# Four K and Q loads moved from the SP queue to GpSimd's queue, between the loads of two weight matrices

## The chip, the cores and the metric

The kernel runs on one core of one Trainium2 chip. The metric is the time of one execution in device microseconds (us), as the median of several runs; the lower the better. The profile shows one execution, in which the hardware profiler recorded every instruction and every DMA packet.

## The reference

Four batches, eight heads, 768 positions and a head size of 64. Causal attention in which every query sees only the six chunks of 32 keys that score highest by a bound, followed by a two-layer network with ELU:

```python
k_min, k_max = k_chunks.min(3), k_chunks.max(3)          # (B, H, 24, D): 24 chunks of 32 keys
ub = sum(maximum(q * k_min, q * k_max), axis=-1)         # bound of every query with every chunk
ub = where(causal, ub, -1e9)
sel = the 6 chunks with the largest ub                   # per query
scores = where(sel & causal, q @ k.T / sqrt(D), -1e9)
x = (softmax(scores) @ v) as (3072, 512)                 # heads side by side
h = x @ w_in                                             # w_in 512 x 2048
out = where(h > 0, h, exp(min(h, 0)) - 1) @ w_out        # w_out 2048 x 512
```

## The kernel before

**Tiling.** The 3072 rows of x are done in eight units of 384. Units 0 and 1 each take 192 positions of batch 0 and the same 192 of batch 1: unit 0 ("p") the positions 0 to 191, for which all chunks that may be seen are among the six, so that no selection is needed, and unit 1 ("s") the positions 192 to 383. The later units are halves of one batch. For each unit the kernel loads K, Q and V, turns K and Q on TensorE (PE), forms minima and maxima of the K chunks (kst) and the bounds, selects, scores, takes exp, multiplies with V, and turns the result into four tiles xt. The two-layer network (`mlp`) of a unit follows: for each of 16 blocks of 128 columns of w_in, four matmuls (L872) accumulate over the four xt; ACT takes exp (L879), GpSimd or DVE subtracts 1 (`m`, L881), DVE joins both sides (`gT`, L885). Then, for three groups of 128 rows, sixteen matmuls with w_out (L896), in four steps of four, one for each piece of w_out.

**The order of work.** Every step is an operation of a graph with a number. The string `ORDER` holds the program's order, written out: three characters for each operation, the first for the engine (P for PE, A for ACT, D for DVE, G for GpSimd, which the profile calls POOL, S for SP) and two for the operation's number. `PLACES` holds the buffer of each tile in the same order. Each engine runs its instructions in this order, and waits on semaphores where an operand isn't ready. SP issues most DMAs; its issues are instructions of its queue as well.

**The loads near the change.** In `prep_pair(b, u, G)` the K and Q rows of one unit come in as two tiles each of class `f` (96 positions x 8 heads x 64 values, float32, 192 KB: 768 runs of 256 bytes), at L308 through the helper `dma`, on SP. Only the Q of unit 0 is loaded by GpSimd, with a cast to bfloat16 (L388). The weights are loaded by GpSimd with a cast as well: w_in in two pieces of eight blocks (`load_w_in`, L295; `GmB` and `GmC` in `ORDER`), w_out in four pieces of four blocks (`load_w_out`, L301; `GmD` to `GmG`). The four loads that the change moves are `S2M` and `S2N` (K) and `S2O` and `S2P` (Q), the cast `G0Y`. The first w_out piece is used by the first L896 of unit 0, the second by the fifth to eighth block, and so on. Everything that GpSimd issues goes through one software queue (q0 in the profile); what SP issues goes through a hardware queue (q1); both are served by the same 16 DMA engines.

**Who uses the moved tiles.** K of unit 1 of batch 1 is turned by PE at L423 (`kT1s0`, `kT1s1`, four transposes each), Q likewise (`qT1s0`, `qT1s1`). The first V tile of batch 1 (128 rows) is cast to bfloat16 into `vext` by GpSimd at L337 (`vcast`). L749 scores unit 1, L613 forms the bounds of all queries with the chunks, L374 is the subtraction of K's minima from the maxima.

Of the kernel before, what the change touches and what calls it, by code (L numbers as in the profile page):

```python
# [34 lines left out]
PE, ACT, DVE, POOL, SP = "PE", "ACT", "DVE", "POOL", "SP"  # L35
# [4 lines left out]
G0vS0UD00D01PjXA02D09PjYS0sPjZG0wD06Pj-D0iPj+S0uPk0G0aPk1D0oS0rPk2A0TD0jG0kPk3A0tPk4S0XD03G04Pk5  # L40
Pk6Pk7Pk8D05G0bP1mD0lG0cG0WP1hP1nPk9S2dG0eG0pG0VPkaPkbPkcP0KA0OD0PPkdPkeG0nG0gG0fS2fPkfPkgD0qD0m
P18P0RP0IG0dD0SD0MP0BS0zA0JA1cP0+P1iD0CS0xA0FD19P1oP1jS0ZD10D1aD13S2eD0LS2gA1qA1pA15D11GmBP16P1f
P1sS2MA1lD0ND0DD0GS2PS2tP1xA1gD17G0AG08G0yP1wA1kD12P1rP1yS2ND0QP1tA1AGmCP1VA1vA1zD0-P1BP1CP1WD1D
P24P23D25A1uG0YP27P28D26G07D1EG1eP1PP1GD29P1QP1-D1XA2aG0EP1ZD1+D20P1MP1FP1LG2hD1HP2bG1bG2QD1RP2z
D1IA1YP2mD2AP1JD2nP2HP21S2GD1ND1OA1SP1TA2qD2oS2OA1KD22P2uD1UA2cPmXG0HG2sA2ID2BG0hD2pG2CPn3AmYDmZ
Dm-Pm+An4PmTGn5An0D2vA2JGmDPmPD2wAmUDbqP3jDn6Gn1Dn2A2DS2RAmQGmVPn7A2rG14D3lA1dPmHG2xAn8D3kD3mGmE
A2yPmLD3nPnfGn9DmWAmMGmRDnaAmIPnDA2KGmNDmSPnrPnzAngGmFD3oA2FAnEGmJDnhPnjD3pGmGDmOA3qA3sPnnDniG3r
AnsP3FDmKAnoGnFPnbA3GGntDnGPnNAnAGnpDnuAncGnBS2kDnqAnkP3+PnvGndA40DnCS2iP3HDneP36D38A3IP2VD37P3Z
# [52 lines left out]
SwSPwJPwKDwLSwMPwVPwWAwXSwYPwZPw-Pw+Px0Dx1Sx2  # L101
"""
PLACES = """
010234561723809400a15670000116732123410154351712367920340512011326120372504022630201740451602060
0001712105100321222310106020041302422105371001210657208104429601a202b10225c63d5074344173e0675174
232002354f0131811a051702149562710202334657702101110353224400271111415003200024301667235013082223
6211124241g0321703025031511642080210211a14023024060172b50d501200217001e9903040645563645270036705
340231510610a143324462420c4518036175460720352160242050221360512703003437015067105025412256406301
2015462720241f034232126300182750369851002011b24115422110702d5117600120301271a12022e1g1502921a044
5364106150341652360311745073a7480420141216521017436560746000200310074351642530340701436007410610  # L110
42322012500347220410676023221c798035120b001246202d1701400505612260110022020f000241743012305621e0
071112221931755412a2640316137544050011601a47135720640203353013120721001117220g041122026531002711
74c02263021d1670105693482300e122f61101154501822304b674310511676271325701101360217051295706272306
123706204523075601020103360271112010022300042411320a621132020237250411ce0252361030170751421bg120
20612350204814010012f010001652733027095310264575302140352735620410026321622347203011031211521200
6712400d341281052302217b02012a13620c211102507243023ef7110g61154420673450256564172631401101225514
# [53 lines left out]
def kernel(  # L170
# [25 lines left out]
    def ap(b):  # L196
        return store[b.cls][b.slot]
# [44 lines left out]
    def short(b):  # L242
        return ap(b)[:, 0:256].bitcast(BF16)
# [61 lines left out]
    def dma(dst_src, writes, reads, name, engines=(SP,)):  # L305
        def emit(e):
            d, s_ = dst_src()
            eng[e].dma_start(out=d, in_=s_)  # L308
        return g.op(name, engines, emit, reads=reads, writes=writes, dma=True)
# [68 lines left out]
    def prep_pair(b, u, G):  # L378
# [4 lines left out]
        if G == 0:  # L383
            for n, cls, src in (("k", "f", k), ("q", "f", q)):
                for x in range(2):
                    ff[b, n, x] = buf = Buf(cls)
                    if (n, u) == ("q", 0):
                        g.op(f"wq{b}{x}", (POOL,), lambda e, buf=buf, x=x: nc.gpsimd.dma_start(  # L388
                            out=short(buf)[0:T96].rearrange("p (h d) -> p h d", d=D),
                            in_=q[b, :, T96 * x:T96 * (x + 1)].rearrange("h p d -> p h d")),  # L390
                            writes=[(buf, i) for i in range(NG)], dma=True)
                        continue
                    for y, (h0, h1) in enumerate(((0, 4), (4, 8)) if (b, u) == (0, 0) else ((0, 8),)):
                        dma(lambda buf=buf, src=src, x=x, h0=h0, h1=h1: (
                                ap(buf)[0:T96, D * h0:D * h1].rearrange("p (h d) -> p h d", d=D),
                                src[b, h0:h1, t0 + T96 * x:t0 + T96 * (x + 1)].rearrange("h p d -> p h d")),
                            [(buf, i) for i in range(h0 // 4, h1 // 4)], [], f"ld{n}{b}{'ps'[u]}{x}{y}",
                            (SP, ACT) if u == 0 and n == "k" else (SP,))
        kf, qf = [[ff[b, n, x] for x in range(2)] for n in "kq"]

        def turned(bk):
# [524 lines left out]
    for u in range(2):  # L926
        for b in range(2):
            for G in range(NG):
                prep_pair(b, u, G)
        if u == 1:  # L930
            for b in range(2):
                select(b, 0)
        else:
            for b in range(2):
                for G in range(NG):
                    score_first(b, G)
        for r in range(NPAIR):
            attend_pair(u, r)
# [63 lines left out]
```

## Time and profile before

| | us |
|---|---|
| median of 3 runs | 280.8 |
| lowest and highest | 280.65 and 281.0 |
| the profiled execution | 280.54 |
| its span, first to last instruction | 278.8 |

The mean TensorE clock granted in the profiled execution was 0.994 of full speed. In the timeline rows the first number is the start in us from the span's start, the second the duration; the bracket at the end tells how long the engine sat idle before it and what ended that. A row of a DMA issue tells the time of the issuing instruction; the time from issue to landing stands in the DMA view, as the last number of a row. In the DMA view the rows of queues tell packets, MB and the time that the packets took as a share of 16 engines' time. In the table by stages each row is a stretch of the span, with the busy time of every engine, the granted clock, and the DMA engines' busy share and rate.

### The profile page before, as it was taken

What the parts mean: (1) busy time and instruction counts of PE and PEld (TensorE: products, weight loads), DVE (VectorE), ACT (ScalarE), POOL (GpSimd) and SP (SyncE); (2) the same over time, 40 slices, a digit from 0 to 9 for tenths busy, and PEclk for the clock granted to TensorE, in tenths of its full rate; (3) what the DMA queues carried; (4) which work ended last, traced back from release to release, by engine and by line L of the source; (5) the groups of instructions that cost most, each with busy time, mean ns of one, the idle gap of its engine ahead of it and who ended that gap; (6) DMA issues with size and microseconds to landing.
All of it is one profiled execution on the core that took longest, in us unless ns stands there. A gap on an engine that the chain in (4) does not pass through costs nothing.

```text
span 278.8 us, 6961 instructions
## 1 busy us (share of the span) xinstructions
PE 266.1 (95%) x2458; PEld 163.2 (59%) x2458; DVE 219.2 (79%) x655; ACT 216.7 (78%) x491; POOL 127.9 (46%) x255
## 2 busy tenths in 40 slices
PE   7587999999999999999999999999999999999995
PEld 4354555785466855576655555666655555665553
DVE  4897976889978999889998999578797698424931
ACT  2577886889699998999999859886968579982620
POOL 8874944258422665321685736212541346310410
PEclk9989999999999999999999999999999999999999
DMA  9999999999228899975965489417600410033002
GB/s 146 203 198 206 229 196 202 224 221 254 49 66 203 238 237 182 209 177 114 195 160 126 104 211 224 77 39 129 173 4 0 60 39 4 14 125 95 16 12 101
DMA packets 103219, 38.07 MB, mean 137 GB/s; under 512 B 95120, under 2 KB 98448, under 8 KB 103184
## 3 DMA queue, kind: packets, MB, share of 16 engines
q1 hardware_dynamic: 95696, 32.75, 56.9%
q0 software_dynamic: 6304, 4.59, 10.7%
q10 hardware_dynamic: 1184, 0.30, 0.5%
q8 instruction: 19, 0.31, 0.5%
q14 instruction: 16, 0.13, 0.2%
HBM read 30.41 MB, written 6.29 MB: 132 GB/s over the span
## 4 chain that ended last, share of the span: by engine, by line
PE 74%; DVE 8%; POOL 5%; ACT 5%; DMA 4%; issue 3%; POOLq 0%; DVEq 0%; ACTq 0%
PE bank L896 26%; PE bank L872 24%; PE bank L803 10%; PE bank L854 5%; DMA w_in_sb<-in_moe_w_in_dram 4%; PE bank L613 3%; PE bank L564 2%; DVE gT L885 2%; ACT pt L818 1%; ACT e L879 1%; PE bank L914 1%; POOL m L881 1%; PE bank L775 1%; POOL f L388 1%; PE bank L749 1%
## 5 line engine op out<-in xcount | busy, mean ns | idle before, releaser
L872 PE MATMUL bank<-xt,w_in_sb 128*128 128x384 bf16 x512 | 89.1, 326 | 1.0 <-DMA w_in_sb<-in_moe_w_in_dram 0.9
L896 PE MATMUL bank<-w_out_sb,gT 128*128 128x512 bf16 x368 | 89.3, 379 | 0.0
L881 POOL TENSOR_SCALAR m<-e 128x384 f32<-128x384 f32 x100 | 52.9, 537 | 61.2 <-ACT e L879 51.1
L885 DVE SCALAR_TENSOR_TENSOR gT<-bank,m 128x384 bf16<-128x384 f32 x128 | 65.7, 549 | 9.5 <-POOL m L881 8.3
L879 ACT ACTIVATE e<-bank 128x384 f32<-128x384 f32 x128 | 59.1, 493 | 15.7 <-PE bank L872 12.9
L872 PEld LDWEIGHTS <-w_in_sb 128*128 128x128 bf16 x512 | 49.3, 98 | 35.6 <-issue 3.1
L818 ACT ACTIVATE pt<-bank 128x384 bf16<-128x384 f32 (+1 forms) x144 | 67.1, 547 | 3.6 <-PE bank L803 2.5
L896 PEld LDWEIGHTS <-gT 128*128 128x128 bf16 x368 | 34.6, 97 | 36.1 <-issue 2.3
L803 PE MATMUL bank<-rhs,lhs 96*128 96x384 bf16 (+2 forms) x240 | 42.8, 293 | 1.0 <-DVE on L667 0.5
L835 POOL TENSOR_TENSOR pt<-pt,tri 128x256 bf16<-128x256 bf16 (+1 forms) x18 | 16.4, 915 | 37.8 <-ACT pt L822 23.9
L803 PEld LDWEIGHTS <-lhs 96*128 96x128 bf16 x240 | 21.7, 97 | 13.9 <-issue 1.0
L854 PEld LDWEIGHTS <-pt 128*128 128x128 bf16 x576 | 21.0, 97 | 3.6 <-ACT pt L818 0.2
L854 PE MATMUL bank<-vext,pt 128*128 128x65 bf16 x576 | 22.1, 193 | 0.0
L667 DVE TENSOR_TENSOR on<-bank,rcp 128x384 bf16<-128x384 f32 (+1 forms) x37 | 18.7, 510 | 1.3
L324 ACT ACTIVATE o<-bank 128x512 f32<-128x512 f32 (+1 forms) x14 | 8.1, 588 | 13.0 <-PE bank L896 10.1
L326 POOL CAST rhs<-qt 64x384 bf16<-64x384 f32 x24 | 12.6, 531 | 12.1 <-ACT qt L324 11.0
L657 DVE RECIPROCAL rcp<-bank 128x6 f32<-128x6 f32 (+1 forms) x40 | 7.2, 185 | 12.5 <-PE bank L854 9.0
L371 DVE TENSOR_REDUCE kst<-bank 128x12 f32<-128x384 f32 x32 | 16.4, 547 | 0.7 <-ACT kt L324 0.4
L326 DVE COPY o<-bank 128x512 f32<-128x512 f32 (+1 forms) x11 | 7.2, 665 | 11.9 <-PE bank L896 9.9
L835 DVE TENSOR_TENSOR pt<-pt,tri 128x512 bf16<-128x512 bf16 (+1 forms) x30 | 11.5, 398 | 5.5 <-ACT pt L822 3.7
L324 ACT ACTIVATE rhs<-qt 64x384 bf16<-64x384 f32 x28 | 14.2, 518 | 0.5
L822 ACT ACTIVATE pt<-bank 128x512 bf16<-128x512 f32 x24 | 14.1, 604 | 0.7 <-PE bank L803 0.5
(105 smaller groups left out, 338.1 us busy)
## 6 DMA issues: line engine op xcount, KB each, us to landing
f<-in_v_dram SPq DMA_DIRECT2D x22, 256.0 KB, 4.6
out_dram<-o SPq DMA_DIRECT2D x21, 256.0 KB, 3.6
f<-in_q_dram SPq DMA_DIRECT2D x18, 256.0 KB, 4.8
f<-in_k_dram SPq DMA_DIRECT2D x18, 256.0 KB, 4.6
kc<-in_k_dram SPq DMA_DIRECT2D x8, 384.0 KB, 4.0
w_in_sb<-in_moe_w_in_dram POOLq DMA_DIRECT2D x2, 1024.0 KB, 12.2
w_out_sb<-in_moe_w_out_dram POOLq DMA_DIRECT2D x4, 512.0 KB, 9.3
f<-in_k_dram SPq DMA_DIRECT2D x5, 192.0 KB, 6.7
```

Of the source, the lines that this page charges most:

```text
L324: nc.scalar.activation(out=dst, in_=src, func=AF.Copy)
L326: eng[e].tensor_copy(out=dst, in_=src)
L667: nc.vector.tensor_tensor(out=ap(on)[:, 0:nt].rearrange("p q h d -> p h q d"), in0=view()[:, :, :, 0:D], in1=ap(rcp)[:, :, 0:nt].to_broadc ...
L803: nc.tensor.matmul(ap(banks[hd])[:, o + pc:o + pc + wd], lhsT=apl(ls, G)[0:96, pr, hd, P * kb:P * (kb + 1)], rhs=ap(rs)[0:96, hd, c0 - HS ...
L818: lambda e, hd=hd, pt=pt, banks=banks, wtot=wtot: nc.scalar.activation(out=ap(pt)[:, hd, PAD:PAD + wtot], in_=ap(banks[hd])[:, 0:wtot], fu ...
L835: eng[e].tensor_tensor(out=view, in0=view, in1=tri[:, 64:64 + P].rearrange("p (a b w) -> p a b w", a=1, b=1) .to_broadcast([P, 2, len(dg), ...
L854: nc.tensor.matmul(view()[:, hd, qi, :], lhsT=ap(pt)[:, hd, P * qi + off:P * qi + off + P], rhs=ap(vx[b])[:, kb, 2 * r + hd, :], start=(kb ...
L872: nc.tensor.matmul(ap(bank)[:, 0:HS], lhsT=w_in_sb[:, kk, P * fc:P * (fc + 1)], rhs=ap(xT[i, kk]), start=(kk == 0), stop=(kk == NKK - 1))
L879: g.op(f"e{i}.{fc}", (ACT,), lambda e, eb=eb, bank=bank: nc.scalar.activation(out=ap(eb), in_=ap(bank)[:, 0:HS], func=AF.Exp), reads=[(ban ...
L881: g.op(f"m{i}.{fc}", (POOL, DVE), lambda e, eb=eb, mb=mb: eng[e].tensor_scalar(out=ap(mb), in0=ap(eb), scalar1=-1.0, scalar2=1.0, op0=AOT. ...
L885: nc.vector.scalar_tensor_tensor(out=ap(gt), in0=ap(bank)[:, 0:HS], scalar=0.0, in1=ap(mb), op0=AOT.max, op1=AOT.min),
L896: nc.tensor.matmul(ap(bank), lhsT=ap(gts[fc])[:, P * tt:P * (tt + 1)], rhs=w_out_sb[:, fc, :], start=(fc == 0), stop=(fc == NFC - 1))
```

## The change

The four loads of K and Q for unit 1 of batch 1 are issued by GpSimd, directly behind its issue of the second w_in piece, K first. The cast of batch 1's first V tile, which GpSimd ran just behind that w_in issue, runs just ahead of it. In SP's order the four issues are gone, and what stood behind them moves up: two copies of constants into `lhs`, then the V loads of unit 1. GpSimd's order around the place is then: first w_in piece, two V casts, the third V cast, second w_in piece, K, K, Q, Q, and on as before. PE, DVE and ACT keep their orders. Some tiles of class `f` change places (`PLACES`), since the loads ask for buffers in another order.

```diff
-P1sS2MA1lD0ND0DD0GS2PS2tP1xA1gD17G0AG08G0yP1wA1kD12P1rP1yS2ND0QP1tA1AGmCP1VA1vA1zD0-P1BP1CP1WD1D
-P24P23D25A1uG0YP27P28D26G07D1EG1eP1PP1GD29P1QP1-D1XA2aG0EP1ZD1+D20P1MP1FP1LG2hD1HP2bG1bG2QD1RP2z
-D1IA1YP2mD2AP1JD2nP2HP21S2GD1ND1OA1SP1TA2qD2oS2OA1KD22P2uD1UA2cPmXG0HG2sA2ID2BG0hD2pG2CPn3AmYDmZ
+P1sA1lD0ND0DD0GS2tP1xA1gD17G0AG08G0yP1wA1kD12P1rP1yD0QP1tA1AG0YGmCG2MG2NG2OG2PP1VA1vA1zD0-P1BP1C
+P1WD1DP24P23D25A1uP27P28D26G07D1EG1eP1PP1GD29P1QP1-D1XA2aG0EP1ZD1+D20P1MP1FP1LG2hD1HP2bG1bG2QD1RP2z
...
-                            (SP, ACT) if u == 0 and n == "k" else (SP,))
+                            (SP, ACT) if (u, n) == (0, "k") else (POOL,) if (b, u) == (1, 1) else (SP,))
```

More of the change, by code (lines that the diff above doesn't have):

```diff
@@ L42 @@
 P18P0RP0IG0dD0SD0MP0BS0zA0JA1cP0+P1iD0CS0xA0FD19P1oP1jS0ZD10D1aD13S2eD0LS2gA1qA1pA15D11GmBP16P1f
-P1sS2MA1lD0ND0DD0GS2PS2tP1xA1gD17G0AG08G0yP1wA1kD12P1rP1yS2ND0QP1tA1AGmCP1VA1vA1zD0-P1BP1CP1WD1D
-P24P23D25A1uG0YP27P28D26G07D1EG1eP1PP1GD29P1QP1-D1XA2aG0EP1ZD1+D20P1MP1FP1LG2hD1HP2bG1bG2QD1RP2z
-D1IA1YP2mD2AP1JD2nP2HP21S2GD1ND1OA1SP1TA2qD2oS2OA1KD22P2uD1UA2cPmXG0HG2sA2ID2BG0hD2pG2CPn3AmYDmZ
+P1sA1lD0ND0DD0GS2tP1xA1gD17G0AG08G0yP1wA1kD12P1rP1yD0QP1tA1AG0YGmCG2MG2NG2OG2PP1VA1vA1zD0-P1BP1C
+P1WD1DP24P23D25A1uP27P28D26G07D1EG1eP1PP1GD29P1QP1-D1XA2aG0EP1ZD1+D20P1MP1FP1LG2hD1HP2bG1bG2QD1R
+P2zD1IA1YP2mD2AP1JD2nP2HP21S2GD1ND1OA1SP1TA2qD2oA1KD22P2uD1UA2cPmXG0HG2sA2ID2BG0hD2pG2CPn3AmYDmZ
 Dm-Pm+An4PmTGn5An0D2vA2JGmDPmPD2wAmUDbqP3jDn6Gn1Dn2A2DS2RAmQGmVPn7A2rG14D3lA1dPmHG2xAn8D3kD3mGmE
@@ L103 @@
 PLACES = """
[L104 to L113, printed above, removed]
+010234561723809400a15670000116732123410154311236725790034051201132612037250402263020174451602060
+0001712105100321222310106020041302422105371001210657208104429601a206b10225c23d5074344173e0675174
+232002354f0131811a051702147562710202334659702101110353224400671111415003200024301267235013082223
+6211124241g0321703025031511642080210211a14023024060172b50d501200217001e7903040645563645270036905
+340231510210a143364462420c4518036175460720352160242050221360512703003437015067105025412256406301
+2015462920241f034232126300182750367851002011b24115422110702d5117600120301271a12022e1g1502921a044
+5364106150341652360311745073a9480420141216521017436560746000200310074351642530340701436007410610
+42322012500349220410676023221c778035120b001246202d1701400505612260110022020f000241743012305621e0
+071112221931755412a2640316137544050011601a47135720640203353013120921001117220g041122026531002711
+74c02263021d1670105673482300e122f61101154501822304b674310511676271325701101360217051295706272306
 123706204523075601020103360271112010022300042411320a621132020237250411ce0252361030170751421bg120
```

## The prediction

> **What bounds the kernel now.** I read the page first, then the table by stages, TensorE's (PE's) waits, its timeline, and last the DMA queues.
>
> ```profile
> span 278.8 us, 6961 instructions
> ...
> PE 266.1 (95%) x2458; PEld 163.2 (59%) x2458; DVE 219.2 (79%) x655; ACT 216.7 (78%) x491; POOL 127.9 (46%) x255
> ```
>
> ```profile
> core 0: us, PE busy (x) PEld busy (x) DVE busy (x) ACT busy (x) POOL busy (x), PEclk, DMA share, GB/s
> 9.88:13.30 3.42, 1.82 (x25) 1.09 (x26) 3.42 (x9) 1.54 (x4) 2.67 (x21) 1.00 1.51 184
> 13.30:16.71 3.41, 3.00 (x24) 1.47 (x23) 3.40 (x8) 2.14 (x5) 3.30 (x7) 0.50 1.36 182
> 20.12:23.54 3.42, 2.14 (x28) 1.76 (x26) 3.13 (x10) 3.27 (x12) 1.84 (x5) 1.00 1.13 205
> 23.74:30.00 6.26, 6.22 (x64) 3.58 (x65) 4.85 (x18) 4.80 (x11) 4.27 (x9) 1.00 1.16 225
> 30.00:35.30 5.30, 5.09 (x33) 2.91 (x31) 5.27 (x18) 4.21 (x11) 4.38 (x8) 1.00 1.27 213
> 35.30:41.30 6.00, 5.35 (x40) 3.04 (x38) 4.95 (x11) 5.26 (x13) 3.38 (x8) 1.00 1.22 196
> 41.30:80.00 38.70, 38.69 (x381) 23.93 (x382) 33.46 (x114) 31.25 (x69) 18.53 (x36) 1.00 0.85 174
> ```
>
> PE is busy 95% of the span. From 23.74 us on it hardly rests: 6.22 of 6.26 us, 5.09 of 5.30, 5.35 of 6.00, then 38.69 of 38.70. A microsecond that PE stands still after 23.74 us is therefore a microsecond of the total, except what can be taken from the 0.65 us that are idle between 35.3 and 41.3.
>
> PE's waits from 23 us to the end hold one row that names a DMA, and the timeline shows where it is:
>
> ```profile
> PE bank L872 <- DMA w_in_sb<-in_moe_w_in_dram: 0.9, 1, 0.9
> ```
>
> ```profile
> 23.78 3.42 PE L872 MATMUL bank<-xt,w_in_sb 128*128 128x384 bf16 x20 [0.87 <-DMA w_in_sb<-in_moe_w_in_dram]
> ...
> 28.09 6.02 PE L872 MATMUL bank<-xt,w_in_sb 128*128 128x384 bf16 x36
> ...
> 34.68 0.81 PE L872 MATMUL bank<-xt,w_in_sb 128*128 128x384 bf16 x4
> 35.33 1.03 PE L896 MATMUL bank<-w_out_sb,gT 128*128 128x512 bf16 x4
> ...
> 37.37 1.08 PE L423 MATMUL bank<-ident_f,f 96*128 96x96 f32 x8
> ...
> 38.72 1.89 PE L896 MATMUL bank<-w_out_sb,gT 128*128 128x512 bf16 x8
> 41.23 0.40 PE L749 MATMUL bank<-rhs,lhs 96*128 96x128 bf16 x3 [0.61 <-ACT lhs L324]
> ...
> 42.55 0.49 PE L423 MATMUL bank<-ident_f,f 96*128 96x96 f32 x4
> ```
>
> The first use of w_in is at 23.78, the first of w_out at 35.33. The eight L423 at 37.37 turn the moved K; those of the moved Q begin at 42.55. Now GpSimd's queue, and the time from issue to landing of each w_in piece and of the first two w_out pieces:
>
> ```profile
> 13.46 0.81 POOL L295 DMA_DIRECT2D w_in_sb<-in_moe_w_in_dram  x1
> ...
> 15.71 0.80 POOL L295 DMA_DIRECT2D w_in_sb<-in_moe_w_in_dram  x1
> 16.54 0.72 POOL L337 TENSOR_SCALAR vext<-f 128x512 bf16<-128x512 f32 x1
> ...
> 18.33 0.21 POOL L374 TENSOR_TENSOR kst<-kst 128x12 f32<-128x12 f32 x1
> ...
> 22.33 0.50 POOL L326 COPY lhs<-kt 64x384 bf16<-64x384 bf16 x1 [1.33 <-ACT kt L324]
> ...
> 26.33 0.83 POOL L301 DMA_DIRECT2D w_out_sb<-in_moe_w_out_dram  x1
> ...
> 29.11 0.78 POOL L301 DMA_DIRECT2D w_out_sb<-in_moe_w_out_dram  x1
> ```
>
> ```profile
> w_in_sb<-in_moe_w_in_dram POOLq DMA_DIRECT2D x1, 1024.0 KB, 10.3
> ...
> w_in_sb<-in_moe_w_in_dram POOLq DMA_DIRECT2D x1, 1024.0 KB, 14.1
> ...
> w_out_sb<-in_moe_w_out_dram POOLq DMA_DIRECT2D x1, 512.0 KB, 8.3
> ...
> w_out_sb<-in_moe_w_out_dram POOLq DMA_DIRECT2D x1, 512.0 KB, 8.9
> ```
>
> Issue plus landing time: w_in at 23.8 and 29.8, w_out at 34.6 and 38.0. They come one after the other, 6.0, 4.8 and 3.4 us apart, though two were issued 2.3 us apart: GpSimd's queue (q0) hands them over in order. The margins are thin. Each block of L872 is four matmuls; the ninth block needs the second w_in piece and starts at 28.09 + 12 x 6.02/36 = 30.1 (piece there 29.8); the first w_out piece is there 0.7 us before its use at 35.33.
>
> **The change part by part.** *Four loads join q0 between w_in and w_out.* Each is 96 x 8 rows of 256 bytes, together 3072 packets. How fast q0 moves such rows beside the SP queue (q1), from the stages at 5 to 7 us and 8 to 11 us (the four Q loads with cast, 256-byte reads), from 18 to 27 us (w_in on q0), and q1 alone from 48 to 55 us:
>
> ```profile
> q0 software_dynamic: 1339, 0.17, 131.4%
> q1 hardware_dynamic: 734, 0.18, 55.7%
> ...
> q0 software_dynamic: 1516, 0.19, 99.8%
> q1 hardware_dynamic: 1771, 0.44, 74.1%
> ...
> q0 software_dynamic: 803, 1.61, 94.5%
> q1 hardware_dynamic: 785, 0.20, 16.9%
> ...
> q1 hardware_dynamic: 6225, 1.57, 105.7%
> ```
>
> q0 got 670 packets per us in the first stage and 505 in the second. 3072 of them take 4.6 or 6.1 us; I take 5.4, the middle, since both rows are the same kind of transfer under the same competition. The ends: alone on the engines at q1's 889 per us, 3.5 us; half of that rate, 6.9 us. q1 will not be empty: while w_in runs it got 785 packets in 9 us, one for each of q0's 803, so whatever SP puts there instead of K and Q is still there at 29.8.
>
> The first w_out piece then lands at 29.8 + 5.4 + 3.4 = 38.6 (3.4 us as between the two pieces that follow each other without a pause; its issue at 26.33 is early enough). PE reaches its L896 at 35.33 as before and stands 3.3 us. Ends: 29.8 + 3.5 + 3.4 = 36.7, a stand of 1.4; 29.8 + 6.9 + 4.8 = 41.5, a stand of 6.2. Behind this L896 in PE's order stand four L872 of the last block, so ACT's exp, GpSimd's m and DVE's gT of that block, and the L423 transposes with DVE's kst and ACT's kt behind them; nothing on PE can pass it.
>
> The Trainium skill speaks for the low end: "DMA: Bandwidth & Descriptors", Queues, rings and completion order, says that an engine takes a whole packet, typically 9 to 17 descriptors, from one ring before it turns to the next, so short rows of q0 would go out many at a turn. By that rule the loads come near the 3.5 us and the sum becomes a stand of 1.4; the rows (803 against 785; 1339 against 734) show at most about two for one, and the rows decide.
>
> *What is late next.* The second w_out piece lands 3.4 later, 42.0. PE asks for it in the second half of the L896 row at 38.72, at 38.72 + 0.95 + 3.3 = 43.0: in time. K (first half of q0's 5.4 us) is there by 32.5, Q by 35.2, against 37.37 and 42.55: in time even without the stand.
>
> *What is won back.* The 0.61 us before L749 at 41.23 are a wait for ACT's copy, which waited for DVE's kst, which waited its turn behind gT work. During the stand DVE empties that work. I take 0.5 back; bounds 0 and 0.65, the stage's whole idle time.
>
> *The clock.* The stretch from 9.88 with PE busy 1.82 of 3.42 us is followed by one at clock 0.50; the stretch from 20.12 with 2.14 busy is not. A stand of 3.3 us lies in two such stretches at most, so one of them has at least 1.65 idle, 1.76 busy, under the first row. A stretch of 3.41 us at half clock loses up to 1.7 us of PE's work; I take 1.2, as part of that stretch is waiting anyway. Bounds 0 (a short stand) and 1.7.
>
> *GpSimd's time.* The four issues cost as the four Q loads at the start did:
>
> ```profile
> L388 POOL DMA_DIRECT2D f<-in_q_dram x4: 772/783/1000, 1.4 to 6.6; - x4
> ```
>
> 4 x 0.78 = 3.1 us from about 17.2. Behind them stand a tri select, lhs copies, the kst subtractions from 18.33 on and small memsets. Before the copy of 22.33 GpSimd waited 1.33 us for ACT, so at most 1.8 of the 3.1 us are left there. The batch-0 bound product on PE, which needs kst, comes after the 20 L872 of 23.78, not before 27.1: room for that. Cost 0; without the cover up to 3.1 us on kst. The Trainium skill, "SBUF — State Buffer", Who interferes with whom, says that DVE in its two-port mode locks GpSimd out of writing descriptors, and the page gives 3.1 us in place of 0.62 for such a transfer; four of these, an estimate by that page, would be 12 us and eat the cover. This trace does not show it: w_in's issues took 0.81 and 0.80 while DVE was busy 3.40 of 3.41 us.
>
> *The V cast ahead of w_in.* 0.72 us (row 16.54), its data there already, since it started without a wait. The second w_in piece is issued 0.7 later, at 16.4, still 7 us before the first has landed, and q0 is in order: cost 0. If q0 ran dry instead: 0.7.
>
> *SP's queue.* Four issues go, among them this one:
>
> ```profile
> 19.71 6.60 SPq L308 DMA_DIRECT2D f<-in_q_dram  x1
> ```
>
> SP reaches the econst copies and V loads up to ten us earlier. They change no PE wait, as none from 23 us on names them: gain 0. Nor does w_in profit much: q1 stays filled, with 256 packets of 768 bytes now first. Were the first piece earlier, PE could not start before its last xt:
>
> ```profile
> 22.78 0.61 DVE L326 COPY xt<-bank 128x384 bf16<-128x384 bf16 x2
> ```
>
> That ends at 23.39, so the gain is at most 0.4 us; slower econst rows may as well cost 0.4. I take 0.
>
> **The sum**: +3.3 - 0.5 + 1.2 = +4.0 us. The profiled execution took 280.54 us (span 278.8 and 1.7 around it), so 284.5; the three runs have their median at 280.8, 0.3 higher: 284.8.
>
> **The rivals.** *No stand to speak of* (chance 0.14): q0's rows go out faster than any row shows, or PE is later than thought; a stand under 1.3 us, no half clock, 0.5 won back: -0.2 to +0.8, about 281.1. Against it: even 889 per us gives 1.4.
>
> *Faster* (0.08): q0 is not strictly in order, the loads slip in beside w_in, and w_out is there by 35.3; then only the 0.4 us at 23.78 count: 280.4. It decides at one point, w_out's landing before 35.3; w_in's landings 6.0 us apart for issues 2.3 apart speak against it.
>
> *GpSimd is held at its own queue* (0.10): SP's issue of 6.60 us shows what a full queue does. With w_in and 3072 rows behind it, GpSimd's third or fourth issue could last until about 26 to 29; kst comes late for the bound product at 27.1 (about 3 us of PE), w_out is issued later still. +6 to +8, about 288. Against it: no GpSimd issue in these rows exceeds 1.0 us, though none had as much queued.
>
> **How the numbers follow.** The forecast has 0.68. Its range: stand 1.4, 0.5 back, no half clock: +0.9, 281.7; stand 4.8 (6.9 us for the loads), nothing back, 1.7 of clock: +6.5, 287.3. I give 281.6 to 287.4, which leaves out the faster case, most of the held queue and part of the first rival, together 2 in 10. 0.2% (0.56 us) is about what a measurement here can tell from no change. Slower by more: 0.68 + 0.10 + 0.07 of the first rival; within: 0.05 of it; faster: 0.08 + 0.02: 0.85, 0.05, 0.10.
>
> **What would show it.** Right: four K and Q rows on GpSimd's DMA issues at about 0.78 us each; the first w_out piece landing some 12 us after issue in place of 8.3; a PE wait of about 3 us at L896 near 35.3, named after w_out's DMA; a half-clock stretch after it; 41 to 80 us as full as now. Wrong: L896 starting at 35.3 without a wait refutes the sum; a long GpSimd issue near 18 to 20 us means the held queue; a long wait at L872 near 30 means that w_in, not w_out, pays.

## The result, and the profile after

| | changed | before |
|---|---|---|
| median of 11 runs, us | 282.46 | 280.92 |
| lowest to highest, us | 281.63 to 285.12 | 280.27 to 281.84 |
| profiled execution, us | 281.63 | 280.54 |

The ratio is 1.0058, 95% interval 1.0038 to 1.0077: slower by 1.5 us, where +4.0 was forecast. The direction and the range held; the size did not. Ratios and intervals here and below come from all executions of both kernels but a few slow ones, so they need not equal the quotient of the medians.

TensorE's (PE's) waits and its timeline of the changed kernel, as in the prediction. The waits' columns are total, times and longest, in us.

```profile
PE bank L896 <- DMA w_out_sb<-in_moe_w_out_dram: 1.7, 1, 1.7
PE bank L872 <- DMA w_in_sb<-in_moe_w_in_dram: 0.9, 1, 0.9
...
PE bank L749 <- ACT lhs L324: 0.6, 1, 0.6
```

```profile
23.32 3.42 PE L872 MATMUL bank<-xt,w_in_sb 128*128 128x384 bf16 x20 [0.86 <-DMA w_in_sb<-in_moe_w_in_dram]
...
36.69 1.02 PE L896 MATMUL bank<-w_out_sb,gT 128*128 128x512 bf16 x4 [1.66 <-DMA w_out_sb<-in_moe_w_out_dram]
...
38.64 0.82 PE L423 MATMUL bank<-ident_f,f 96*128 96x96 f32 x8
...
42.25 0.40 PE L749 MATMUL bank<-rhs,lhs 96*128 96x128 bf16 x3 [0.61 <-ACT lhs L324]
```

The new wait is where the prediction put it: the first L896, ended by the first w_out piece. It lasts 1.66 us, not 3.3. The 0.61 us before the later L749 has stayed. And PE begins L872 0.46 us earlier than in the execution of before (23.32 against 23.78).

The rows of GpSimd's DMA issues, by the DMA view; the last number is the median time from issue to landing. The first row is of the second w_in piece, the last of the first w_out piece.

```profile
w_in_sb<-in_moe_w_in_dram POOLq DMA_DIRECT2D x1, 1024.0 KB, 12.8
f<-in_k_dram POOLq DMA_DIRECT2D x2, 192.0 KB, 13.1
f<-in_q_dram POOLq DMA_DIRECT2D x2, 192.0 KB, 13.7
...
w_out_sb<-in_moe_w_out_dram POOLq DMA_DIRECT2D x1, 512.0 KB, 10.8
```

And GpSimd's timeline:

```profile
16.30 0.79 POOL L295 DMA_DIRECT2D w_in_sb<-in_moe_w_in_dram  x1
17.10 1.58 POOL L308 DMA_DIRECT2D f<-in_k_dram  x2
18.67 1.54 POOL L308 DMA_DIRECT2D f<-in_q_dram  x2
...
22.12 0.95 POOL L326 COPY lhs<-kt 64x384 bf16<-64x384 bf16 x2
```

The four issues took 3.12 us (3.1 predicted), and at 22.12 GpSimd is level with before: nothing was paid there. The second w_in piece lands at 16.30 + 12.8 = 29.1, the four loads by 33.3 (single landings 30.1, 31.2, 32.2, 33.3), the first w_out piece at 36.6. So, by the landings, the loads took 4.2 us, not 5.4, and were complete one by one in order, 1.05 us apart.

Why they were faster shows in the table of queues of the page (packets, MB, share). First the changed kernel's row, then that of before:

```profile
q0 software_dynamic: 6560, 5.37, 12.0%
```

```profile
q0 software_dynamic: 6304, 4.59, 10.7%
```

The four loads brought 0.78 MB in 256 more packets, not 3072. Of those, by the packet records, 192 carry 4096 bytes, sixteen rows of 256 bytes each, and 64 are of 4 bytes. The packets of 4096 bytes start between 27.4 and 32.1 us, the first of them before w_in has landed, and w_out's first one starts at 31.7. In the stretch in which q0 sent hardly anything else (28.6 to 30.6 us), SP's rows, still one per packet, went out one for each packet of q0:

```profile
q0 software_dynamic: 129, 0.39, 94.1%
q1 hardware_dynamic: 127, 0.03, 13.3%
```

So the two queues took turns packet by packet, as beside w_in in the prediction (803 against 785). But a packet of the loads held 4096 bytes and one of q1 256: q0 moved 0.39 MB beside 0.03 MB on q1.

No half-clock stretch follows the wait. The profiler's stretches of 3.41 us around it, in the columns of the table by stages, and the later stage:

```profile
32.80:36.21 3.41, 1.99 (x13) 0.96 (x11) 3.01 (x7) 2.88 (x7) 2.45 (x6) 1.00 1.21 195
36.21:39.62 3.41, 2.94 (x27) 2.19 (x27) 1.79 (x4) 2.02 (x5) 1.47 (x3) 1.00 1.22 196
...
41.30:80.00 38.70, 38.07 (x378) 23.50 (x377) 33.10 (x112) 31.20 (x68) 18.57 (x36) 1.00 0.87 176
```

From 42 us on the kernel runs 1.0 us behind before, and ends 1.1 behind (279.9 against 278.8). The 0.6 us that the last row has less than before (38.07 for 38.69) are the wait ahead of L749, which now falls into this stage.

### The profile page after: what moved, and what is told of

It is laid out like the page before. It is cut to its first block, busy times and chain, and to the rows that moved or that the text cites. A ratio compares the mean times of both kernels' runs of the same rounds, so it can differ in the third digit from the quotient of the medians.

```text
span 279.9 us, 6961 instructions
## 1 busy us (share of the span) xinstructions
PE 263.9 (94%) x2458; PEld 162.6 (58%) x2458; DVE 218.5 (78%) x655; ACT 216.7 (77%) x491; POOL 130.8 (47%) x259
## 2 busy tenths in 40 slices
DMA packets 100339, 38.07 MB, mean 136 GB/s; under 512 B 92048, under 2 KB 95376, under 8 KB 100304
## 4 chain that ended last, share of the span: by engine, by line
PE 74%; DMA 9%; DVE 6%; POOL 4%; ACT 3%; issue 2%; POOLq 0%; DVEq 0%; ACTq 0%
PE bank L896 26%; PE bank L872 24%; PE bank L803 10%; PE bank L854 5%; DMA w_out_sb<-in_moe_w_out_dram 4%; DMA w_in_sb<-in_moe_w_in_dram 4%; PE bank L613 3%; PE bank L564 2%; DMA kc<-in_k_dram 2%; ACT e L879 1%; PE bank L914 1%; PE bank L749 1%; PE bank L775 1%; DVE kn L514 1%; POOL f L388 1%
## 5 line engine op out<-in xcount | busy, mean ns | idle before, releaser
L896 PE MATMUL bank<-w_out_sb,gT 128*128 128x512 bf16 x368 | 89.3, 379 | 1.7 <-DMA w_out_sb<-in_moe_w_out_dram 1.7
L872 PE MATMUL bank<-xt,w_in_sb 128*128 128x384 bf16 x512 | 89.0, 326 | 0.9 <-DMA w_in_sb<-in_moe_w_in_dram 0.9
L872 PEld LDWEIGHTS <-w_in_sb 128*128 128x128 bf16 x512 | 49.3, 98 | 35.5 <-issue 3.0
L896 PEld LDWEIGHTS <-gT 128*128 128x128 bf16 x368 | 34.6, 97 | 37.9 <-issue 4.1
L835 POOL TENSOR_TENSOR pt<-pt,tri 128x256 bf16<-128x256 bf16 (+1 forms) x18 | 16.6, 924 | 38.4 <-ACT pt L822 23.6
L835 DVE TENSOR_TENSOR pt<-pt,tri 128x512 bf16<-128x512 bf16 (+1 forms) x30 | 10.8, 376 | 5.5 <-ACT pt L822 3.7
```

What stands on the lines that cost most here:

```text
L835: eng[e].tensor_tensor(out=view, in0=view, in1=tri[:, 64:64 + P].rearrange("p (a b w) -> p a b w", a=1, b=1) .to_broadcast([P, 2, len(dg), ...
L872: nc.tensor.matmul(ap(bank)[:, 0:HS], lhsT=w_in_sb[:, kk, P * fc:P * (fc + 1)], rhs=ap(xT[i, kk]), start=(kk == 0), stop=(kk == NKK - 1))
L896: nc.tensor.matmul(ap(bank), lhsT=ap(gts[fc])[:, P * tt:P * (tt + 1)], rhs=w_out_sb[:, fc, :], start=(fc == 0), stop=(fc == NFC - 1))
```

## The experiments

Theory A is the prediction's: the cost is the late first w_out piece. Theory B: GpSimd's time or order costs it. Theory C of the expectations: half-clock stretches cost it. No such stretch follows the wait in either trace of the changed kernel, so C falls there. Theory D: a second wait, near 97 us in the changed kernel, is part of the price. With the result came a further question, called the packing below: were the loads faster than forecast because q0 sends sixteen rows in a packet? In the diffs a token is one operation of `ORDER`; G is GpSimd's place, S is SP's; `mC` is the second w_in piece, `mD` the first w_out piece, `2M`, `2N` the K loads, `2O`, `2P` the Q loads, `0Y` the V cast. The first four kernels shared their runs of before (median 282.0 us).

**Only K on GpSimd.**

```diff
-G0YGmCG2MG2NG2OG2P
+G0YGmCG2MG2NS2OS2P
```

> Only the two K loads go through GpSimd behind w_in; the two Q loads are issued by SP at the same place of the order. Theory A (the loss is the late first w_out piece, and each of these loads costs q0 about 1.05 us, as the four landed at 30.1, 31.2, 32.2 and 33.3 us in the trace after): w_out lands at about 34.5 us, PE is ready for it at about 34.9, no wait at L896, and the earlier start of PE (23.3 instead of 23.8 us) stays: 280.2 to 280.8 us, at or 0.2% under the kernel before. Theory B (the loss comes from GpSimd's 3.1 us of issuing and what stands behind it): half of it stays, about 281.7 us. Theory C (it comes from the half-clock stretches, 0.98 to 1.0 mean clock in the runs after): nothing to do with the number of loads, about 282 us.

Measured: 282.36 us, ratio 1.0034 (1.0001 to 1.0067). The first w_out piece lands 6.3 us after the second w_in piece (7.5 in the changed kernel, 4.9 before). Its waits:

```profile
PE bank L690 <- DVE on L667: 2.2, 2, 1.6
...
PE bank L896 <- DMA w_out_sb<-in_moe_w_out_dram: 0.6, 1, 0.6
```

Half the loads, a third of the wait. A expected no wait, with w_out at 34.5 us; it landed at 36.1, as w_in came 0.7 us later and w_out 4.0 us behind the second K load in place of 3.4. The time is above what A expected, and B's (281.7, 0.3% over before) fits it as well, so this run alone doesn't part A from B. The 1.6 us are at L690 near 97 us: theory D's wait, larger here than in the first trace of the changed kernel (0.55).

**The first w_out piece ahead of the loads.**

```diff
-G0YGmCG2MG2NG2OG2P ... GmD
+G0YGmCGmDG2MG2NG2OG2P
```

> All four loads stay on GpSimd, but the first w_out piece is issued between w_in and them. Theory A: the first w_out piece lands at about 32.6 us, no wait at the first L896; the second lands at 29.2 + 3.4 + 4.2 + 3.4 = 40.2 us and PE asks for it at about 39.2: a wait of 1.0 us there instead of 1.7, total about 281.3 us. Theory B: GpSimd issues as much as in the changed kernel, earlier even: 282.5 us. Theory C: no change from 282.5 us.

Measured: 281.03 us, ratio 0.9966 (0.9938 to 0.9993). The four loads are still on GpSimd, with their four issues 0.9 us later, and the first L896 doesn't wait. The second w_out piece lands at 40.2 and is waited for, both as A expected, in the second half of the same loop:

```profile
40.27 1.02 PE L896 MATMUL bank<-w_out_sb,gT 128*128 128x512 bf16 x4 [1.09 <-DMA w_out_sb<-in_moe_w_out_dram]
```

So B falls: GpSimd issues as much as in the changed kernel, only w_out's piece goes ahead of the loads on q0, and the kernel is faster than before.

**Loads and w_out pieces interleaved.**

```diff
-G0YGmCG2MG2NG2OG2P ... GmD ... GmE
+G0YGmCGmDG2MG2NGmEG2OG2P
```

> GpSimd issues w_in, first w_out piece, K, K, second w_out piece, Q, Q, and the last two w_out pieces as before. Theory A: first w_out piece at 32.6, K by 34.7 (asked for at 37), second w_out piece at 38.1 (asked for at 39.2), Q by 40.2 (asked for at 42), third piece at 43.6 (asked for at about 44): no wait, the earlier start of PE stays, about 280.4 us. Theory B: 282.5 us or more, as GpSimd issues two w_out pieces earlier as well. Theory C: 282.5 us.

Measured: 280.79 us, ratio 0.9947 (0.992 to 0.9974). No wait for w_out is left. It was run once more, on other runs of before (median 281.95 us):

> The interleaved order (second w_in piece, first w_out piece, K, K, second w_out piece, Q, Q) once more, on another set of runs of the kernel before. If its gain over the kernel before is real, the ratio lies again between 0.992 and 0.998 and no wait on a DMA stands at L896; if it was a scatter of the chip it lies between 0.998 and 1.003. The wait near 97 us, 1.20 us in the first run of this order, should lie again over 0.8 us if the order of the loads decides it, anywhere between 0 and 1.7 if it is scatter.

Measured: 280.44 us, ratio 0.9957 (0.9925 to 0.999). Both runs agree: this order beats both kernels.

**The four loads at the same place, but on SP.**

```diff
-G0YGmCG2MG2NG2OG2P
+G0YGmCS2MS2NS2OS2P
```

> The order of the changed kernel, with the V cast ahead of w_in, but SP issues the four loads, at the same place of the order (behind the first econst copy, ahead of the V loads). Theory A: q0 carries only weights as in the kernel before, so w_out lands at about 34.5 us and L896 does not wait; if the earlier landing of the first w_in piece came from econst standing ahead of K in SP's queue, it stays (23.3 us), if from K and Q being gone from that queue, it goes (23.8 us): 280.4 or 280.9 us. Theory B: GpSimd's time is free again, 280.9 us. Theory C: about 282 us.

Measured: 281.09 us, ratio 0.9963 (0.9938 to 0.9989). This is faster than before, though none of the four loads went to GpSimd: SP only issues the four loads later, and the constants earlier. The timeline shows the gain at the start of the network, where PE no longer waits for w_in at all but for its last xt:

```profile
23.45 3.56 PE L872 MATMUL bank<-xt,w_in_sb 128*128 128x384 bf16 x20 [0.27 <-DVE xt L326]
```

What ends sooner is SP's stream of 256-byte rows ahead of w_in. The queues from 14.5 to 16.5 us in the kernel before (first fence) and in this one (second), with w_in's first piece issued at 13.46 in both:

```profile
q1 hardware_dynamic: 1380, 0.35, 124.0%
q0 software_dynamic: 18, 0.04, 11.5%
```

```profile
q1 hardware_dynamic: 792, 0.20, 65.2%
q0 software_dynamic: 36, 0.07, 54.3%
```

**Only the V cast moved.** Before, with `GmC` and `G0Y` changed round.

```diff
-AGmC ... G0Y
+AG0YGmC
```

> The kernel before with only the V cast moved ahead of the second w_in issue; the four loads stay with SP at their old places. Theory A (the time of the change is the lateness of the first w_out piece behind the four loads): w_in lands as before, near 23.5 and 29.6, w_out near 34.6, no wait at the first L896, ratio to before 0.998 to 1.002. Rival: the cast's 0.7 us delays the second w_in piece by as much, and with it w_out; then w_in lands at 30.4, PE waits 0.3 us at the ninth block of L872, and the ratio is 1.001 to 1.003. What a second rival (the wait near 97 us is caused by the new order of GpSimd's work) expects here: that wait is there only where the loads are on GpSimd, so under 0.5 us here.

Measured: 282.22 us, ratio 1.0004 (0.9975 to 1.0033). No cost of the cast shows: the second w_in piece lands 5.9 us behind the first (6.0 before), the ninth block of L872 doesn't wait, and the interval allows 0.8 us to either side. Nor is the gain of the kernel above the cast's as far as this run shows: w_in lands at 24.6 here, later than the 23.5 expected, and the wait near 97 us is 1.21 us, though no load is on GpSimd.

**The changed kernel again**, beside the next two, which shared its runs of before (median 281.4 us).

> The changed kernel once more, on the chip of the runs beside it. Theory A (the loss is the wait for the first w_out piece, less what PE starts earlier): 0.3 to 0.8% over the kernel before, a wait of 1.3 to 2.0 us at the first L896, and the four loads landing 1.0 to 1.1 us apart. Theory D (a second loss sits at about 96 us, where DVE waits for a kc load and PE for DVE: 0.55 us in the first trace after, 1.2 to 1.6 in three of the four kernels so far): that wait appears again, 0.4 to 1.6 us. Theory C (half-clock stretches after the wait): a stretch at clock 0.5 between 36 and 45 us.

Measured: 283.14 us, ratio 1.0057 (1.0028 to 1.0087). The loads land 1.0 to 1.1 us apart and the wait at the first L896 is 1.65 us, both as A expected; the one near 97 us is 1.66. The first lies this time inside one stretch of the clock, and no half clock follows it:

```profile
34.88:38.29 3.41, 1.76 (x12) 0.91 (x11) 2.54 (x6) 2.35 (x7) 2.47 (x5) 1.00 1.22 196
38.29:41.70 3.41, 3.41 (x29) 2.20 (x26) 2.28 (x5) 2.53 (x5) 0.90 (x3) 1.00 1.21 195
```

**Six loads in place of four.** Two K loads of batch 3 more, into buffers that nobody reads yet; their data isn't used.

```diff
-G0YGmCG2MG2NG2OG2P
+G0YGmCG2MG2NG2OG2PGx3Gx4
...
+    for x in range(2):
+        g.op(f"extra{x}", (POOL,), lambda e, x=x: nc.gpsimd.dma_start(
+            out=store["o"][x][0:T96].rearrange("p (h d) -> p h d", d=D),
+            in_=k[3, :, T96 * x:T96 * (x + 1)].rearrange("h p d -> p h d")), dma=True)
```

> Two further K loads of the same shape (batch 3, into buffers that nothing else uses yet; the result is not changed) are issued by GpSimd behind the four. Theory A: each adds 1.05 us to q0; the first w_out piece lands at about 38.8 us and the wait at L896 is about 3.7 us instead of 1.7; total 2.1 us over the changed kernel, 1.3% over the kernel before. Theory C: an idle time of that length brings a half-clock stretch as well, 3.0 to 3.8 us over the changed kernel. Theory B (GpSimd's time): 1.6 us more of issuing, the kst subtractions late at about 22.7 to 25.3 us, still ahead of L613: no wait there either, so no more than the changed kernel.

Measured: 286.11 us, ratio 1.0156 (1.0116 to 1.0196). The six land 1.0 to 1.15 us apart and w_out at 38.6, when L896 starts. Its wait is 2.12 us, put down to DVE:

```profile
38.62 1.02 PE L896 MATMUL bank<-w_out_sb,gT 128*128 128x512 bf16 x4 [2.12 <-DVE gT L885]
```

```profile
21.06:24.48 3.42, 1.46 (x13) 1.02 (x14) 2.05 (x6) 1.83 (x6) 3.01 (x10) 1.00 1.13 206
24.48:27.89 3.41, 3.41 (x13) 1.53 (x12) 2.56 (x6) 1.72 (x4) 2.43 (x6) 0.50 1.13 212
```

w_out landed at 38.58 (38.8 expected by A), just ahead of the start, and DVE had long been done: the transfer ended last in fact. The wait is shorter than the 3.7 us expected because PE came late. The two rows of the table by stages show why PE came to it only at 36.5: a stretch with PE busy for 1.46 us, while it waited for w_in, then one at half clock. A part of this kernel's extra time is that, not the two loads.

**The Q loads with a cast to bfloat16**, as unit 0 has them; the packets then are 128-byte rows. Q is rounded, and PE turns it as bfloat16.

```diff
-                                ap(buf)[0:T96, D * h0:D * h1].rearrange("p (h d) -> p h d", d=D),
+                                (short(buf) if (n, b, u) == ("q", 1, 1) else ap(buf))[0:T96, D * h0:D * h1].rearrange("p (h d) -> p h d", d=D),
```

> The two Q loads of the changed kernel's four are made with a cast to bfloat16, as those of unit 0 are, and turned as bfloat16; the selection of batch 1 is made from rounded Q values. Theory A with packing (loads without a cast leave q0 in packets of 4096 bytes, 48 for each load, as the packet sizes in the trace after say, and with a cast row by row, 128 bytes each): 768 packets for each Q load, 1.2 to 1.5 us apart instead of 1.05, the first w_out piece 0.3 to 0.9 us later than in the changed kernel, and q1's rate while the Q loads run rises from some 64 packets per us to several hundred. Theory A without packing (the rate is set by bytes or by HBM): Q loads land 1.0 us apart or less, as they write half the bytes, and q1's rate stays under 100 packets per us.

Measured: 285.4 us, ratio 1.0114 (1.0069 to 1.016). The Q loads land 1.7 us apart (1.2 to 1.5 expected by the packing), where the K loads ahead of them land 0.8 apart. The queues while q0 sends mostly the Q loads' packets (29.3 to 31.3 us):

```profile
q0 software_dynamic: 736, 0.13, 77.6%
q1 hardware_dynamic: 745, 0.19, 71.8%
```

The turns are one packet for one again, but a packet of the Q loads holds 128 bytes, and half the bytes of a load without a cast take longer: the packing holds. The cast by itself isn't what slows them: w_in has one too, in packets of 2048 bytes, and q0 moved 1.61 MB of it in 9 us, again beside q1 (the prediction's row of 803 packets). The wait in the timeline, and the clock behind it in the table by stages:

```profile
38.12 1.86 PE L896 MATMUL bank<-w_out_sb,gT 128*128 128x512 bf16 x4 [2.72 <-DMA w_out_sb<-in_moe_w_out_dram]
```

```profile
33.95:37.36 3.41, 1.23 (x8) 0.67 (x8) 2.79 (x7) 3.27 (x8) 2.58 (x6) 1.00 1.22 195
37.36:40.77 3.41, 2.65 (x9) 1.24 (x9) 0.80 (x2) 0.32 (x1) 0.71 (x2) 0.50 1.21 210
40.77:44.18 3.41, 3.41 (x21) 2.91 (x20) 1.38 (x3) 1.71 (x4) 0.21 (x2) 0.50 1.21 203
```

This is what the prediction forecast for the changed kernel, a wait of about 3 us and half clock behind it; it needs the slower loads. From the start of L896 to the L423 of K it takes 3.79 us (1.95 in the changed kernel), so the clock cost 1.8.

**The kernel before, three more profiled executions**, one time each (283.45, 282.88 and 282.4 us; no ratio).

> The kernel before once more, for a second trace. Theory D in its strong form (the change brings the wait at 96 us about): no wait there, as in the first trace before. In its weak form (the kc load lands now in time, now not, in either kernel): a wait of 0 to 1.6 us there. The first w_in piece lands at 23.7 us, plus or minus 0.3, if that time is a matter of the order of SP's queue; if it moves by more, the earlier start of PE after the change (0.46 us) is no more than its scatter.

> The kernel before, one more profiled execution, for two things that the sum took as nothing. First, the landing of the first w_in piece: 23.7 and 25.4 us in the two executions of this kernel so far and 24.6 with the V cast alone moved, against 23.3 to 24.0 in the seven kernels whose K and Q loads had left their old places on SP. If those loads delay w_in, it lands again at 24.0 or later; if it is scatter, anywhere from 23.3 to 25.4. Second, the wait near 97 us (0 and 0.47 us in this kernel so far, 0.4 to 1.7 in the others): if the V cast or the moved loads cause it, it stays under 0.5; if it is scatter, it may be over 1.

> The kernel before, a further profiled execution, for the same two questions: the first w_in piece at 24.0 us or later and a wait near 97 us under 0.5 us, if the moved loads and the V cast decide them; the first anywhere from 23.3 and the second up to 1.7 us if both are scatter.

Measured: the first w_in piece lands at 25.4, 24.7 and 24.1 us; the wait near 97 us is 0.47, 0.56 and 1.25 us. The last of the three has, in its waits,

```profile
PE bank L690 <- DVE on L667: 1.9, 2, 1.2
```

So the kernel before has theory D's wait too. It is DVE's `kn` (L505), which waits for a K load of the next unit and holds up the `on` behind it; over all fourteen executions it is 0 to 1.7 us, with and without the change. The change doesn't bring it about. Whether it makes it longer these runs don't show: the mean is 0.6 us over the four executions of before and 1.1 over the two of the changed kernel.

On w_in the expectations disagree: 25.4 lies outside 23.7 plus or minus 0.3, which the first of them took as a sign of scatter, while all three lie at 24.0 or later, as the other two expect if the loads at their old places delay w_in. The traces together speak for the delay. With the loads at their old places on SP (four executions of before, and the kernel with the V cast alone) w_in landed at 23.7, 24.1, 24.6, 24.7 and 25.4, mean 24.5; in the eight executions without K and Q there, at 23.3 to 24.0, mean 23.6 (23.8 with only K moved to GpSimd). The first of w_in's packets of 2048 bytes started at 15.6 to 16.1 us in the five and at 15.0 to 15.4 in the nine others. Where both kinds ran in one set on one chip, 25.4 stands against 23.4 to 23.7, and 24.6 against 23.5. And two of the five had a half-clock stretch after the longer wait for w_in (six loads had one too):

```profile
21.43:24.84 3.41, 1.25 (x16) 0.88 (x14) 2.49 (x8) 2.29 (x8) 1.28 (x3) 1.00 1.13 206
24.84:28.25 3.41, 3.41 (x12) 1.61 (x12) 1.48 (x4) 0.98 (x2) 0.21 (x1) 0.50 1.13 215
```

## Why the prediction was right or wrong

**Right:** the mechanism and its place. GpSimd's queue hands its transfers over in order; w_out lands late behind the four loads; PE stands at the first L896; and 0, 2, 4 and 6 loads put w_out's first landing 4.9, 6.3, 7.5 and 8.7 us behind the second w_in piece. Putting w_out first removes the stand. Right too: GpSimd's issue time (3.12 us) at cost 0, the V cast at 0 (1.0004, though the interval reaches 0.8 us), K and Q in time for their L423, the second w_out piece in time once PE had stood. The rivals "GpSimd held at its own queue" (1.58 and 1.54 us for two issues each) and "Faster" (w_out at 36.6, not before 35.3) didn't come.

**The step that failed: the rate of the four loads, and with it the stand.** The prediction counted 3072 packets, one for each 256-byte row, and took 505 to 670 packets per us from the rows of the Q loads at the start. Those loads have a cast, and go out as one small packet per row; the four moved loads have none, and went out sixteen rows at a time. The prediction weighed the Trainium skill's rule ("DMA: Bandwidth & Descriptors", Queues, rings and completion order: an engine takes a whole packet, typically 9 to 17 descriptors, before it turns to another ring) and put its rows above it. The rule was right here, with 16 rows in a packet and 129 packets of q0 against 127 of q1. The rows it lost to were sound, but of another form of transfer; the kernel with the cast shows both in one trace, 0.8 us for a load without the cast, 1.7 with it.

Of the 1.6 us by which the stand came short, the loads make 1.2 (4.2 for 5.4). The second w_in piece landed 0.7 earlier than assumed (29.1 for 29.8), the time behind the loads made 0.1, and PE came 0.3 earlier (35.0 for 35.3), which took 0.3 back. So it is partly luck that the low end's stand of 1.4, which rests on 3.5 us for the loads, is close to 1.66.

Each load added only some 0.6 us to w_out's landing, though it takes 1.05. In the kernel before, and with the loads on SP, w_out's first landing comes 4.7 to 5.3 us after w_in's second, in the kernels that issue it early 3.4 to 3.5. So some 1.4 us of pause on q0 stood before w_out. In the kernel before it shows from 29.1 to 29.5 us, 2.8 us after w_out's issue:

```profile
q1 hardware_dynamic: 336, 0.10, 124.1%
q0 software_dynamic: 1, 0.00, 0.3%
```

The loads filled it by and by: from the last transfer ahead of it to w_out's landing it took 4.9, 4.0, 3.3 and 2.6 us with 0, 2, 4 and 6 loads. The prediction added 3.4 us behind the loads and the changed kernel has 3.3 (36.6 less 33.3); since this time isn't fixed, that is luck as well. The cause of the pause stays open.

**The clock, +1.2, was 0.** It hung on the stand of 3.3. The threshold taken from the row with 1.82 us of PE busy was also too high here: 1.76 (the changed kernel again) and 1.99 brought no half clock, 1.46, 1.25 and 1.23 did. Near the start, though, stretches with 1.54 to 2.03 us busy (beginning at 7.4 to 10.6 us, in twelve of the fourteen traces) were followed by half clock, so between some 1.5 and 2.0 us PE's busy time alone doesn't settle it. The Trainium skill, "TensorE: Matmul & The Clock Gate", What's actually happening, gives an idle window of about 3.4 us as the condition; the window's length agrees with the 3.41 us, but it need not be wholly idle: 1.46 us of work in one did not keep the clock up.

**Won back, -0.5, was 0.** The 0.61 us before L749 came back unchanged in the changed kernel and in those with K alone, with the loads on SP, interleaved, and with six loads. The stand ahead of it doesn't shorten the chain through kst and ACT: the chain begins with the L423 of K, which stand behind the stand in PE's order, and from their end to L749 it takes 2.8 us in both traces (38.45 to 41.23 before, 39.46 to 42.25 changed). It vanished with w_out first, where PE stood 1.09 us just ahead of it, and with the cast, where half clock had slowed PE.

**SP's queue, 0, was about -1.0.** The prediction looked at what SP reaches sooner, and not at what it no longer has in flight when w_in starts. With the loads out of the way w_in begins and lands sooner, PE starts L872 0.9 us earlier in the mean (23.6 against 24.5), and a half-clock stretch behind the wait there came in one execution of eight in place of two of five. The kernel with the loads on SP at the new place shows it without the stand: 0.9963, or -1.0 us (0.3 to 1.7). The prediction's bound of 0.4 came from the one execution that it had, in which w_in landed earlier than in any other of that kernel.

Added up with what was measured: +1.66 for the stand, 0 for the clock, 0 won back, -1.0 for w_in: +0.7, against +1.5 measured (interval 1.1 to 2.2). The remaining 0.8 us lies within the intervals of the two ratios it is built from (0.5 and 0.7 us to a side) and wasn't located; the wait near 97 us, 0.5 longer in the mean of the changed kernel's two executions than in the four of before, may be a part. In the two profiled executions side by side PE started 0.46 us earlier, stood 1.66, and ended 1.1 later.

## What to carry to other kernels

Before a transfer is moved into an in-order queue, see what is next in that queue and when it is needed; here the same four loads cost 0.6% ahead of w_out and gained 0.4 to 0.5% interleaved behind its first pieces. Nearly all of that gain may come from where they left: issued by SP at the later place, they gained 0.4% too. Take a queue's rate only from transfers of the same form (cast or none, same row length), count its packets and the bytes in one, and ask what the old queue gains, too: a load taken away from the stretch before a large transfer can be worth as much as the stall it causes elsewhere. Where the margin is under a microsecond, one trace of the kernel before isn't enough: w_in's landing ranged over 1.6 us in four executions.

## What the runs showed of the hardware

- With work on both, the software queue and SP's took turns packet by packet, whatever the size: 803 against 785 (2048 bytes against mostly 256), 129 against 127 (4096), 736 against 745 (mostly 128). In the prediction's two rows from the start, 1339 against 734 and 1516 against 1771, it was not one for one.
- Loads without a cast left the software queue as 4096-byte packets of sixteen 256-byte rows (48 for a load of 192 KB) at 0.7 to 1.2 us a load by the landings; with a cast to bfloat16 the same rows went as 768 packets of 128 bytes, at 1.7 us a load. SP's queue sent its 256-byte rows one by one in every trace.
- Between 20 and 270 us, a stretch of 3.41 us with PE busy for 1.46 us or less was followed by one or two at half clock (four times, after 0.63, 1.23, 1.25 and 1.46 us), one with 1.76 us or more by none; near the start stretches with 1.54 to 2.03 us were followed by half clock too.
- The pause on the software queue ahead of w_out (w_out 4.7 to 5.3 us behind w_in in place of 3.4 to 3.5) was there although w_out had been issued 2.1 to 3.6 us before w_in landed; issued at 17 us it was gone.
